# First product of two experts in the second token part: seven products of halves in place of eight

## The chip, the core and the metric

The program runs on one core of a Trainium2 chip. The metric is the device time of one execution in microseconds (us); before the change the median of three runs is 1135.14 us (1130.4 to 1138.75). The engines named here are PE (TensorE, the matmuls), DVE (VectorE), ACT (ScalarE), POOL (GpSimd) and SP (the queue that issues the transfers).

## What is computed

Attention over 4 batches and 8 heads gives a matrix `x` of 2304 tokens by 512. Then four experts and a last block work on it:

```python
p = domain_probs / (domain_probs.sum(-1, keepdims=True) + 1e-09)
out = np.zeros((N, D), dtype=np.float32)
for e in range(E):                       # 4 experts
    h = np.maximum(x @ w1[e], 0.0)       # first product, 512 -> 1024
    out += p[:, e:e + 1] * (h @ w2[e])   # second product, 1024 -> 512
# then: h = x @ w_in; SoLU and layer norm; @ w_out
```

## The kernel before

The 2304 tokens are 18 tiles of 128. Tiles 0 to 5 are the first part, tiles 6 to 17 the second; the second part is cut into four groups of three tiles, 384 tokens each (`GROUPS`). Every matrix is held as two f16 pieces, a high and a low one, and a product of two matrices is three matmuls: high times high, high times low, low times high.

The experts run in phases `j` = 0 to 7: phases 0 to 3 are the four experts on the first part, 4 to 7 the four experts on the second. Phases 0 to 4 run beside the attention, which ends in phase 4. Phase 5 is the second expert and phase 6 the third, both on the second part; phase 7 is the fourth, and the last block follows.

One group of one phase is two stretches. In the first, `emit_h` (matmul in line 310) makes 8 chunks of 128 hidden units by 384 tokens, each 4 slices of the inner dimension times three matmuls: 96 matmuls of 384 columns. A chunk has a PSUM bank (tile `hps`); ACT takes its positive part into the high half of a tile `hch` (line 318), and DVE writes the low half (line 319). In the second stretch `emit_o` (line 330) makes, for each of three token tiles, 24 matmuls of 512 columns into a bank `ops`, and DVE adds the result into `acc` (line 354; in the first expert ACT writes it, line 349, with a small scale `c` that DVE makes in line 374 into one of three buffers).

The weights of phase j+1 are loaded and split in phase j: `next_w` returns the loads and the splits, four of each per matrix (ACT line 263, DVE line 266, 1024 columns each), and `spread` mixes them among the units of a phase. The weights of the last block, `w_in` and `w_out`, come as 64-bit words, so DVE first turns them into 32-bit floats (lines 189 to 213) in buffers of a pool `cv`; a sum of their squares then goes through a small reduction (DVE line 246, matmul line 248).

A scheduler orders the instructions of each engine from this program order and from priorities (`tc.high_priority`); each engine then works in its order. PSUM has 8 banks: 3 in the pool `psh` and, from phase 5 on, 5 in the pool `psb`, taken in turn.

Of the kernel before, what the change touches and what calls it, by code (L numbers as in the profile page):

```python
# [14 lines left out]
AF = mybir.ActivationFunctionType  # L15
ALU = mybir.AluOpType
# [3 lines left out]
NB, NH, S, HD = 4, 8, 576, 64  # L20
NT, D, F, E = 2304, 512, 1024, 4
KD, KF = D // 128, F // 128
# [3 lines left out]
PRI = 2000  # L26
# [14 lines left out]
GROUPS = [[(0, 3), (3, 3)], [(6, 3), (9, 3), (12, 3), (15, 3)]]  # L41
NACC = 6
GT = 3
# [15 lines left out]
def tile_kernel(  # L59
# [16 lines left out]
    pe = nc.tensor  # L76
# [21 lines left out]
    vec, act, gp, sync = nc.vector, nc.scalar, nc.gpsimd, InOrder(nc.sync)  # L98
# [7 lines left out]
    hp = ctx.enter_context(tc.tile_pool(name="h", bufs=8))  # L106
# [51 lines left out]
    wt = {}  # L158
    cv = {}
# [129 lines left out]
    xT, x2T, acc = {}, {}, {}  # L289
# [9 lines left out]
    def emit_h(e, t0, k, fs, pool):  # L299

        g, c0 = group(t0)
        n = 128 * k
        ps = pool.tile([128, 512], F32, tag="h", name="hps")
        w, x = wt["w1", e], xT[g]
        h = hp.tile([128, 2, 128 * GT], F16, tag="h", name="hch")
        for j, f in enumerate(fs):
            m = 0
# [14 lines left out]

    def emit_o(e, o0, pool):

        ps = pool.tile([128, 512], F32, tag="h", name="ops")
        w = wt["w2", e]
        m = 0
        for f in range(KF):
            for a, b in ((0, 0), (0, 1), (1, 0)):
                pe.matmul(  # L330
                    ps, hch[f][:, a, o0:o0 + 128], w[:, b, f, :], start=(m == 0), stop=(m == 3 * KF - 1)
                )
                m += 1
        return ps
# [66 lines left out]
    def phase_units(j, runs, pool):  # L401

        e = j % E
        units = []
        for t0, k in runs:
            cost = 12 * (k * 128 / 2400 + 0.003)
            per = GT // k
            for f in range(0, KF, per):
                fs = range(f, min(f + per, KF))
                units.append((t0 + k - 1, lambda t=t0, k=k, fs=fs: emit_h(e, t, k, fs, pool), cost * len(fs)))  # L410
            for t in range(t0, t0 + k):
                units.append((
                    t, lambda t=t, o=(t - t0) * 128: out_unit(e, t, o, pool), 24 * 0.216,
                ))
        return units


    nw = [0]
# [619 lines left out]
    late.append(ctx.enter_context(tc.tile_pool(name="late", bufs=1)))  # L1038
    fetch()


    psbs = ExitStack()
    psb = psbs.enter_context(tc.tile_pool(name="psb", bufs=8 - NPH, space=PSUM))
    for j in range(5, 8):
        us = phase_units(j, GROUPS[1], psb)
        n = len(us) if j < 7 else len(us) * 3 // 4
        with ExitStack() as es:
            if j == 7:
                cv["pool"] = es.enter_context(tc.tile_pool(name="cv", bufs=2))
            pa, qa = next_w()  # L1050
            pb, qb = next_w()
            end = 0.9 * n if j < 7 else n
            for _, u, _ in spread(us[:n], (0, 0.1 * n, post), (0.1 * n, 0.5 * n, pa + qa), (0.5 * n, end, pb)):
                u()
        post = qb
    m = len(us) - n
    for _, u, _ in spread(us[n:], (m - 3.0, m - 0.5, post)):
        u()
# [170 lines left out]
```

## Time and profile before

| what | value |
|---|---|
| median of the runs | 1135.14 us |
| the profiled execution, its own time | 1134.88 us |
| its span, first to last instruction | 1132.9 us |
| outside of the span | 2.0 us |
| PE busy | 1072.2 us, 95% of the span |
| DVE busy | 708.8 us, 63% |
| ACT busy | 470.2 us, 42% |
| POOL busy | 184.5 us, 16%, none of it after about 430 us |
| first product (line 310) | 396.9 us of PE |
| second product (line 330) | 387.4 us of PE |
| phase 5 begins, phase 6 begins, phase 7 begins | 569.43, 692.20, 816.76 us |

Busy time counts the time in which an engine had an instruction running. "x" and a number is how many instructions a row puts together. "idle before" is the idle time of the engine ahead of these instructions, with what ended it.

### The profile page before, as it was taken

The page shows a single profiled execution, that of the slowest core. Times are in us where ns is not written, and L with a number is a line of the kernel's source. Part 1 is how long each engine was busy: PE and PEld are TensorE (multiplying, and loading weights), DVE is VectorE, ACT ScalarE, POOL GpSimd, SP SyncE. Part 2 cuts the span into 40 slices and gives each one's busy share as a digit, 9 for nine tenths or more (in the row PEclk, how much of TensorE's full clock was granted, in tenths as well). Part 3 has the DMA queues.
Part 4 walks back from the last instruction along what each step waited for, and adds up shares of the span by engine and source line. Part 5 has one row for each costly group of instructions (what it writes and reads, how often), then busy time and mean ns, then how long its engine had stood idle before and what let it go on. Part 6 is the DMA issues. An engine that isn't in the chain of part 4 may idle for free.

```text
span 1132.9 us, 18415 instructions
## 1 busy us (share of the span) xinstructions
PE 1072.2 (95%) x7200; PEld 608.7 (54%) x7200; DVE 708.8 (63%) x1530; ACT 470.2 (42%) x1003; POOL 184.5 (16%) x176
## 2 busy tenths in 40 slices
PE   4588889899998999999999999999999999999998
PEld 4456766466555656655555555555555554444443
DVE  7898778557677678535332225212788656999883
ACT  5566776646655466432321123111334342333222
POOL 4974633224125311000000000000000000000000
PEclk9999989899999999999999999999999999999999
DMA  9777986738649547324240004000232102343433
GB/s 322 218 170 160 239 200 156 218 81 230 155 95 267 135 127 194 73 42 138 80 144 1 1 1 149 1 1 1 76 93 84 37 21 29 75 103 75 84 84 84
DMA packets 216054, 125.75 MB, mean 111 GB/s; under 512 B 183712, under 2 KB 185760, under 8 KB 215456
## 3 DMA queue, kind: packets, MB, share of 16 engines
q1 hardware_dynamic: 215968, 124.59, 42.7%
q8 instruction: 56, 0.92, 0.3%
q14 instruction: 30, 0.25, 0.1%
HBM read 73.18 MB, written 6.29 MB: 70 GB/s over the span
## 4 chain that ended last, share of the span: by engine, by line
PE 78%; DMA 9%; DVE 5%; POOL 4%; issue 2%; ACT 1%; SPq 1%; POOLq 0%; ACTq 0%; DVEq 0%
PE ops L330 29%; PE hps L310 27%; PE h L1080 8%; PE o L1143 8%; DMA pT<-hl 6%; PE pv L683 2%; PE sps L610 1%; DMA vraw<-in_vC_dram 1%; DVE hl L654 1%; PE sps L611 1%; DVE nm L616 1%; POOL ks L493 1%; POOL wt L259 1%; ACT p L649 1%; POOL ks L491 1%
## 5 line engine op out<-in xcount | busy, mean ns | idle before, releaser
L310 PE MATMUL hps<-xT,wt 128*128 128x384 f16 (+1 forms) x2688 | 396.9, 307 | 2.2 <-DVE hch L319 1.2
L330 PE MATMUL ops<-wt,hch 128*128 128x512 f16 x1728 | 387.4, 381 | 2.5 <-DVE hch L319 1.3
L310 PEld LDWEIGHTS <-wt 128*128 128x128 f16 x2688 | 240.9, 100 | 137.7 <-issue 5.5
L330 PEld LDWEIGHTS <-hch 128*128 128x128 f16 x1728 | 167.4, 99 | 195.7 <-issue 6.5
L318 ACT ACTIVATE hch<-hps 128x384 f16<-128x384 f32 (+1 forms) x194 | 93.8, 484 | 257.5 <-PE hps L310 257.1
L319 DVE SCALAR_TENSOR_TENSOR hch<-hps,hch 128x384 f16<-128x384 f32 (+1 forms) x194 | 105.9, 548 | 124.2 <-ACT hch L318 124.1
L649 ACT ACTIVATE p<-sps,nm 128x320 f32<-128x320 f32 (+4 forms) x144 | 79.0, 553 | 88.5 <-DVE nm L620 55.2
L654 DVE TENSOR_TENSOR hl<-p,hl 128x320 f16<-128x320 f32 (+4 forms) x132 | 91.8, 708 | 30.3 <-ACT hl L653 30.0
L266 DVE SCALAR_TENSOR_TENSOR wt<-stage,ws,wt 128x1024 f16<-128x1024 f32 x72 | 97.0, 1367 | 21.2 <-ACT wt L263 19.8
L354 DVE SCALAR_TENSOR_TENSOR acc<-ops,coef,acc 128x512 f32<-128x512 f32 x54 | 40.4, 748 | 111.0 <-PE ops L330 111.0
L1080 PE MATMUL h<-wt,x2T 128*128 128x512 f16 x432 | 95.5, 379 | 0.8 <-DVE acc L354 0.8
L1143 PE MATMUL o<-wt,lt 128*128 128x512 f16 x432 | 95.5, 379 | 0.0
L610 PE MATMUL sps<-ks,qhi 128*128 128x288 f32 (+3 forms) x160 | 67.4, 424 | 19.0 <-ACT p L649 8.8
L263 ACT ACTIVATE wt<-stage,ws 128x1024 f16<-128x1024 f32 x64 | 70.6, 1141 | 16.0 <-PE ops L330 11.2
L683 PE MATMUL pv<-v,pT 128*128 128x64 f16 x1392 | 54.7, 197 | 17.2 <-DMA pT<-hl 17.2
L1080 PEld LDWEIGHTS <-x2T 128*128 128x128 f16 x432 | 42.2, 98 | 52.0 <-issue 1.1
L1143 PEld LDWEIGHTS <-lt 128*128 128x128 f16 x432 | 42.3, 98 | 50.9
L653 ACT ACTIVATE hl<-p 128x320 f16<-128x320 f32 (+4 forms) x132 | 65.9, 521 | 6.9 <-DMA pT<-hl 6.4
L683 PEld LDWEIGHTS <-pT 128*128 128x128 f16 x1392 | 49.5, 100 | 26.6 <-DMA pT<-hl 21.0
L1093 ACT ACTIVATE ex<-h,nb,cs 128x1024 f32<-128x1024 f32 x18 | 21.7, 1205 | 84.4 <-DVE nb L1090 43.6
L611 PE MATMUL sps<-ks,qlo 128*128 128x288 f32 (+3 forms) x160 | 52.2, 329 | 3.1 <-POOL qlo L493 3.1
L127 ACT ACTIVATE junk<-stage 128x1024 bf16<-128x1024 f32 x40 | 42.1, 1053 | 25.7 <-DMA stage<-in_w_dram 12.9
(130 smaller groups left out, 939.5 us busy)
## 6 DMA issues: line engine op xcount, KB each, us to landing
stage<-in_w_dram SPq DMA_DIRECT2D x64, 512.0 KB, 5.8
raw<-in_qT_dram SPq DMA_DIRECT2D x34, 256.0 KB, 3.6
vraw<-in_vC_dram SPq DMA_DIRECT2D x30, 256.0 KB, 3.2
raw<-in_kT_dram SPq DMA_DIRECT2D x24, 288.0 KB, 3.6
raw<-in_w_in_dram SPq DMA_DIRECT2D x4, 1024.0 KB, 6.0
raw<-in_w_out_dram SPq DMA_DIRECT2D x4, 1024.0 KB, 5.2
out_dram<-o2s SPq DMA_DIRECT2D x16, 256.0 KB, 2.0
raw<-in_kT_dram SPq DMA_DIRECT2D x8, 192.0 KB, 4.2
```

Of the source, the lines that this page charges most:

```text
L263: h = bg_(act.activation(out=hi, in_=r, func=AF.Copy, scale=stage[key, "s"]), "A")
L266: stage["last"] = vec.scalar_tensor_tensor(out=lo, in0=r, scalar=stage[key, "s"], in1=hi, op0=ALU.mult, op1=ALU.subtract)
L310: pe.matmul(ps[:, j * n:j * n + n], w[:, a, kk, f * 128:(f + 1) * 128], x[:, b * KD + kk, c0:c0 + n], start=(m == 0), stop=(m == 3 * KD - 1),)
L318: nc.scalar.activation(out=h[:, 0, :n], in_=ps[:, :n], func=AF.Relu)
L319: nc.vector.scalar_tensor_tensor(out=h[:, 1, :n], in0=ps[:, :n], scalar=0.0, in1=h[:, 0, :n], op0=ALU.max, op1=ALU.subtract)
L330: pe.matmul(ps, hch[f][:, a, o0:o0 + 128], w[:, b, f, :], start=(m == 0), stop=(m == 3 * KF - 1))
L610: pe.matmul(o, hi[:, h % 4], rhs, start=True, stop=False)
L649: act.activation(out=dst, in_=src, func=AF.Exp, bias=nm[:, j + x:j + x + 1], scale=SCALE, accum_out=sums[:, h:h + 1],)
L654: anc["D"] = vec.tensor_tensor(out=hl[:, W + c0:W + c0 + n_], in0=pf[:, 0:n_], in1=hl[:, c0:c0 + n_], op=ALU.subtract)
L683: pe.matmul(o, tt[:, a * nch + c, :], v[:, bb, hs], start=(m == 0), stop=(m == total - 1))
L1080: pe.matmul(ps[:, half], x[:, a * KD + kk, c:c + 128], w[:, b, kk, half * 512:half * 512 + 512], start=(m == 0), stop=(m == 3 * KD - 1),)
L1143: pe.matmul(ps, tt[:, a * KF + f], w[:, b, f], start=(m == 0), stop=(m == 3 * KF - 1))
```

## The change

In phases 5 and 6 the first product of a group, (1024 hidden by 512 inner) times (512 inner by 384 tokens), is cut in halves in all three dimensions and done by Strassen's scheme in Winograd's form: seven products of 512 by 256 by 192 in place of eight, with sums of halves ahead of them and behind them. Phase 7, phases 0 to 4 and all second products stay as they are.

- The hidden dimension is taken in two passes (`half` 0 and 1). A pass has seven products (`f1` to `f7`), each in one bank: 2 column halves `jj`, 2 inner slices, 3 matmuls, so 12 matmuls of 192 columns; a group has 14 products and 168 matmuls.
- Behind the products, `add` (DVE, seven per pass, 384 columns) and one ACT copy put them together in f32 tiles `stu` in SBUF; `hidden` takes the positive part (ACT, 192 columns, 8 per pass) and the low piece (DVE, 8 per pass).
- Ahead of the products, `t_steps` makes four sums `T` of the token halves, once per group of tokens, and `s_steps` four sums `S` of the weight halves, once per expert and pass. Each is 14 DVE instructions (384 columns for `T`, 512 for `S`) and 4 ACT copies. The sums of group 0 and of the second expert are put among the units that are left of phase 4 when the attention has been issued; `T` of the other groups and `S` of the third expert stand in phase 5.
- `T` and `S` lie in a pool `keep` and the f32 tiles in a pool `tmp`, both closed after phase 6; the pool `cv` is opened only then.
- The second products take the chunks in the order in which they were made (`for f in hch`), and in phases 5 and 6 their banks come from `psh`.

```diff
+    def combine(shape, out, x, y, op):
+        ...
+        def high():
+            r["f"] = view(st_["tmp"].tile([128, 512], F32, tag="f", name="stf", bufs=3))
+            vec.tensor_tensor(out=r["f"], in0=x(0), in1=y(0), op=op)
+
+        def low():
+            if y(1) is None:
+                vec.tensor_tensor(out=r["f"], in0=r["f"], in1=x(1), op=ALU.add)
+                return
+            if "l" not in r:
+                r["l"] = view(st_["tmp"].tile([128, 512], F32, tag="l", name="stl", bufs=1))
+                vec.tensor_tensor(out=r["l"], in0=x(1), in1=y(1), op=op)
+            vec.tensor_tensor(out=r["f"], in0=r["f"], in1=r["l"], op=ALU.add)
+
+        def split():
+            two_parts(r["f"], out(0), out(1))     # ACT copy to f16, DVE subtract
+        return r, [high, low, split]
+
+    def st_units(e, g, half, pool):
+        ...
+        def product(c, lhs, rhs):
+            ps[c] = pool.tile([128, 512], F32, tag="h", name="hps")
+            for jj in range(2):
+                m = 0
+                for kk in range(2):
+                    for a, b in ((0, 0), (0, 1), (1, 0)):
+                        pe.matmul(
+                            ps[c][:, jj * HT:jj * HT + HT], lhs(a, kk, jj), rhs(b, kk),
+                            start=(m == 0), stop=(m == 5),
+                        )
+                        m += 1
+        def add(k, x, y):
+            ...
+                vec.tensor_tensor(out=u[k], in0=x, in1=y, op=ALU.add)
+        def hidden(x, fs, j):
+            ...
+                    act.activation(out=h[:, 0], in_=v, func=AF.Relu)
+                    vec.scalar_tensor_tensor(
+                        out=h[:, 1], in0=v, scalar=0.0, in1=h[:, 0], op0=ALU.max, op1=ALU.subtract
+                    )
+        def f1():
+            ...
+            product(1, A(0, 0), B(0, 0))
+            ...
+                act.activation(out=u["b"], in_=ps[1][:, :W], func=AF.Copy)
+        def f2():
+            product(6, S(1), T(1))
+            add("u", u["b"], ps[6][:, :W])
+        def f3():
+            product(2, A(0, 1), B(1, 0))
+            add("s1", u["b"], ps[2][:, :W])
+            hidden(u["s1"], fa, 0)
+        def f4():
+            product(7, S(2), T(2))
+            add("v", u["u"], ps[7][:, :W])
+        def f5():
+            product(5, S(0), T(0))
+            add("s2", u["v"], ps[5][:, :W])
+            hidden(u["s2"], fb, 1)
+            add("w", u["u"], ps[5][:, :W])
+        def f6():
+            product(4, A(1, 1), T(3))
+            add("s3", u["v"], ps[4][:, :W])
+            hidden(u["s3"], fb, 0)
+        def f7():
+            product(3, S(3), B(1, 1))
+            add("s4", u["w"], ps[3][:, :W])
+            hidden(u["s4"], fa, 1)
+    ...
-        for f in range(KF):
+        for f in hch:
...
-    while moe:
-        moe.pop()[1]()
...
+    for _, u, _ in spread(moe, (0, len(moe), t_steps(0) + s_steps(1, 0) + s_steps(1, 1))):
+        u()
...
-    for j in range(5, 8):
-        us = phase_units(j, GROUPS[1], psb)
+    for j in (5, 6):
+        ...
+        tasks = [post + pa[:5], pa[5:] + qa, [], pb]
+        if first:
+            for g in range(3):
+                tasks[g] = t_steps(g + 1) + tasks[g]
+        for _, u, _ in st_phase(e, psb, psh, tasks, [s_steps(e + 1, h) for h in range(2)] if first else None):
+            u()
+    sts.close()
+    us = phase_units(7, GROUPS[1], psb)
```

On PE, at the head of the first group of phase 5, a chunk of the kernel before is 12 pairs of a weight load and a matmul of 384 columns (`hps` is the bank, `wt` the weights, `xT` the tokens; `ops_7415` is the last second product of phase 4):

```order
L330 MATMUL ops_7415<-wt_6128,hch_7336 128x512
L310 LDWEIGHTS wt_6684
L310 MATMUL hps_7473<-xT_2313,wt_6684 128x384
L310 LDWEIGHTS wt_6684
L310 MATMUL hps_7489<-xT_2313,wt_6684 128x384
```

In the changed kernel, at the ninth product of the same group (of 12 pairs of 192 columns), there stands:

```order
L529 LDWEIGHTS S_7356
L529 MATMUL hps_7718<-T_7046,S_7356 128x192
L331 LDWEIGHTS hch_7554
L331 MATMUL ops_7844<-wt_7774,hch_7554 128x512
...
L331 LDWEIGHTS hch_7555
L331 MATMUL ops_7844<-wt_7774,hch_7555 128x512
L529 LDWEIGHTS wt_6684
L529 MATMUL hps_7738<-xT_2313,wt_6684 128x192
```

The matmuls are half as wide, and in this first group some of the second product's matmuls (`ops_7844`, six here) stand between the first products.

On DVE, behind the last chunk `hch_7149` of phase 4's third group, the kernel before has the conversion of `w_in` and then that of the next chunks (`cvA`, `cvP` are its words). The changed kernel has there the sums of group 0 (`stf`, `stl` are the f32 tiles, `xT_2313` the tokens of group 0, `T_7046` their sums):

```order
L320 SCALAR_TENSOR_TENSOR hch_7149<-hps_7148,hch_7149 128x384
L437 TENSOR_TENSOR stf_7063<-xT_2313 128x384
L445 TENSOR_TENSOR stl_7065<-xT_2313 128x384
L446 TENSOR_TENSOR stf_7063<-stf_7063,stl_7065 128x384
L437 TENSOR_TENSOR stf_7090<-xT_2313,stf_7063 128x384
L445 TENSOR_TENSOR stl_7166<-xT_2313 128x384
L425 TENSOR_TENSOR T_7046<-stf_7063,T_7046 128x384
L441 TENSOR_TENSOR stf_7090<-stf_7090,xT_2313 128x384
L437 TENSOR_TENSOR stf_7127<-xT_2313,stf_7090 128x384
L437 TENSOR_TENSOR stf_7164<-xT_2313 128x384
L425 TENSOR_TENSOR T_7046<-stf_7090,T_7046 128x384
L441 TENSOR_TENSOR stf_7127<-stf_7127,xT_2313 128x384
```

Four rows on comes the first of three small scales (`c0`, line 374 before), then the sums of the second expert's weights. The conversion of `w_in` has moved behind phase 6.

On DVE, further on in phase 5's first group, the adds that empty the banks (`stu<-stu,hps`) stand among the sums of the last group (`T_8349`, tokens `xT_6125`) and the splits of the third expert's first weights (`wt_8209`):

```order
L548 SCALAR_TENSOR_TENSOR hch_7555<-stu_7602,hch_7555 128x192
L541 TENSOR_TENSOR stu_7643<-stu_7626,hps_7630 128x384
L541 TENSOR_TENSOR stu_7649<-stu_7586,hps_7630 128x384
L541 TENSOR_TENSOR stu_7667<-stu_7626,hps_7654 128x384
L266 SCALAR_TENSOR_TENSOR wt_8209<-stage_7870,ws_7872,wt_8209 128x1024
L425 TENSOR_TENSOR T_8349<-stf_8450,T_8349 128x384
L441 TENSOR_TENSOR stf_8504<-stf_8504,xT_6125 128x384
L266 SCALAR_TENSOR_TENSOR wt_8209<-stage_7870,ws_7872,wt_8209 128x1024
L446 TENSOR_TENSOR stf_8594<-stf_8594,stl_8622 128x384
L266 SCALAR_TENSOR_TENSOR wt_8209<-stage_7870,ws_7872,wt_8209 128x1024
L541 TENSOR_TENSOR stu_7688<-stu_7649,hps_7675 128x384
L541 TENSOR_TENSOR stu_7731<-stu_7714,hps_7718 128x384
```

Before the change DVE had there only the eight chunks of the group and four splits. `hps_7675` is the seventh product of the group; the twelfth, `hps_7775`, takes its bank.

## Rows read from the trace of the kernel before

**Rows 1.** The page: busy time, and the slices of PE, DVE and the granted clock.
```profile
PE 1072.2 (95%) x7200; PEld 608.7 (54%) x7200; DVE 708.8 (63%) x1530; ACT 470.2 (42%) x1003; POOL 184.5 (16%) x176
...
PE   4588889899998999999999999999999999999998
...
DVE  7898778557677678535332225212788656999883
...
PEclk9999989899999999999999999999999999999999
```

**Rows 2.** Busy time in phases 5, 6, 7: PE, PEld, DVE, ACT, POOL, clock.
```profile
569.40:692.20 122.80, 122.80 (x662) 64.69 (x661) 35.35 (x52) 24.35 (x41) 0.00 (x0) 1.00 0.13 42
692.20:816.80 124.60, 124.60 (x674) 65.77 (x673) 42.83 (x59) 26.20 (x44) 0.00 (x0) 1.00 0.09 34
816.80:942.60 125.80, 124.96 (x677) 66.15 (x676) 88.55 (x159) 45.53 (x85) 0.00 (x0) 1.00 0.22 58
```

**Rows 3.** Timeline of PE: start, length, line, form, count.
```profile
537.32 16.74 PE L310 MATMUL hps<-xT,wt 128*128 128x384 f16 x102
553.89 15.70 PE L330 MATMUL ops<-wt,hch 128*128 128x512 f16 x72
569.43 13.98 PE L310 MATMUL hps<-xT,wt 128*128 128x384 f16 x85
...
692.20 15.76 PE L310 MATMUL hps<-xT,wt 128*128 128x384 f16 x96
707.80 15.70 PE L330 MATMUL ops<-wt,hch 128*128 128x512 f16 x72
723.34 15.76 PE L310 MATMUL hps<-xT,wt 128*128 128x384 f16 x96
```

**Rows 4.** Timeline of PE: runs of short matmuls beside the attention.
```profile
98.09 5.25 PE L310 MATMUL hps<-xT,wt 128*128 128x128 f16 x91
...
370.74 1.04 PE L683 MATMUL pv<-v,pT 128*128 128x64 f16 x30
```

**Rows 5.** Groups of PE and its weight loads: count, busy us, mean ns of one.
```profile
L310 PE MATMUL hps<-xT,wt 128*128 128x128 f16 x576 | 41.3, 232 | 1.0 <-DMA xT<-xh 1.0
L310 PEld LDWEIGHTS <-wt 128*128 128x128 f16 x2688 | 240.9, 100 | 137.7 <-issue 5.5
L683 PEld LDWEIGHTS <-pT 128*128 128x128 f16 x1392 | 49.5, 100 | 26.6 <-DMA pT<-hl 21.0 <-issue 0.9
```

**Rows 6.** Groups of DVE and ACT by form: count, busy us, mean ns.
```profile
L319 DVE SCALAR_TENSOR_TENSOR hch<-hps,hch 128x384 f16<-128x384 f32 x188 | 103.5, 553 | 124.2 <-ACT hch L318 124.1
L213 DVE TENSOR_TENSOR stage<-stage,cvA 128x1024 f32<-128x1024 f32 x8 | 9.6, 1217 | 0.0
L318 ACT ACTIVATE hch<-hps 128x384 f16<-128x384 f32 x188 | 91.5, 487 | 256.7 <-PE hps L310 256.4
L393 ACT ACTIVATE xh<-acc,xs 128x512 f16<-128x512 f32 x18 | 12.9, 717 | 6.7 <-DVE xs L138 5.4 <-DVE xi L131 1.4
```

**Rows 7.** Timeline of DVE in phase 7, where instructions follow without a gap.
```profile
859.84 2.47 DVE L266 SCALAR_TENSOR_TENSOR wt<-stage,ws,wt 128x1024 f16<-128x1024 f32 x2
862.23 1.01 DVE L319 SCALAR_TENSOR_TENSOR hch<-hps,hch 128x384 f16<-128x384 f32 x2
...
865.89 2.35 DVE L213 TENSOR_TENSOR stage<-stage,cvA 128x1024 f32<-128x1024 f32 x2
868.16 1.67 DVE L236 TENSOR_SCALAR stage<-stage,gl 128x512 f32<-128x512 f32 x4
```

**Rows 8.** Timeline of ACT and DVE around the end of the attention.
```profile
520.36 0.69 DVE L189 TENSOR_SCALAR cvA<-raw 128x1024 int32<-128x1024 int32 x1 [0.94 <-DMA raw<-in_w_in_dram]
...
521.16 0.49 ACT L318 ACTIVATE hch<-hps 128x384 f16<-128x384 f32 x1 [1.46 <-PE hps L310]
...
529.03 0.69 DVE L205 TENSOR_SCALAR cvP<-cvA 128x1024 int32<-128x1024 int32 x1
...
538.29 0.27 DVE L374 TENSOR_SCALAR c<-pt,iw 128x1 f32<-128x1 f32 x1 [4.96 <-ACT acc L349]
```

**Rows 9.** Timeline of DVE and PE in phase 7: the reduction of `w_in`.
```profile
833.73 0.15 DVE L246 TENSOR_REDUCE wt<-wt 128x1 f32<-128x4 f32 x1
...
853.75 0.28 PE L248 MATMUL tp<-wt,ones 128*128 128x1 f32 x2
```

More of the change, by code (lines that the diff above doesn't have):

```diff
@@ L306, in emit_h @@
         for j, f in enumerate(fs):
+            hch.pop(f, None)
             m = 0
@@ L415, in phase_units, with two_parts, view @@
         return units
+    HT = 64 * GT
+    st_ = {}
+    Ts, Ss = {}, {}
+    def two_parts(x, hi, lo):
+        act.activation(out=hi, in_=x, func=AF.Copy)
+        vec.tensor_tensor(out=lo, in0=x, in1=hi, op=ALU.subtract)
+    def combine(shape, out, x, y, op):
+        n = shape[0] * shape[1]
+        r = {}
+        def view(f):
+            return f[:, :n].rearrange("p (a b) -> p a b", a=shape[0])
+        def high():
[12 more added lines that the diff above has]
+        return r, [high, low, split]
@@ new lines, in t_steps, with B, T, place @@
+    def t_steps(g):
+        X = xT[1, g]
+        def B(i, j):
+            return lambda b: X[:, b * KD + 2 * i:b * KD + 2 * i + 2, HT * j:HT * j + HT]
+        def T(k):
+            return lambda b: Ts[g][:, k, b]
+        def place():
+            Ts[g] = st_["keep"].tile([128, 4, 2, 2, HT], F16, tag=f"T{g}", name="T")
+        sh = (2, HT)
+        r1, a1 = combine(sh, T(0), B(0, 1), B(0, 0), ALU.subtract)
+        r2, a2 = combine(sh, T(1), B(1, 1), lambda b: None if b else r1["f"], ALU.subtract)
+        r3, a3 = combine(sh, T(2), B(1, 1), B(0, 1), ALU.subtract)
+        r4, a4 = combine(sh, T(3), B(1, 0), lambda b: None if b else r2["f"], ALU.subtract)
+        return [place] + a1 + a2 + a4 + a3
@@ new lines, in s_steps, with A, S, place @@
+    def s_steps(e, half):
+        def A(i, j):
+            return lambda b: wt["w1", e][:, b, 2 * j:2 * j + 2, 512 * i + 256 * half:512 * i + 256 * half + 256]
+        def S(k):
+            return lambda b: Ss[e, half][:, k, b]
+        def place():
+            Ss[e, half] = st_["keep"].tile([128, 4, 2, 2, 256], F16, tag=f"S{half}", name="S")
+        sh = (2, 256)
+        r1, a1 = combine(sh, S(0), A(1, 0), A(1, 1), ALU.add)
+        neg = lambda b: None if b else r1["f"]
+        r2 = {}
+        def second():
+            r2["f"] = st_["tmp"].tile([128, 512], F32, tag="f", name="stf", bufs=3).rearrange("p (a b) -> p a b", a=2)
+            vec.tensor_tensor(out=r2["f"], in0=r1["f"], in1=A(0, 0)(0), op=ALU.subtract)
+        def second_low():
+            vec.tensor_tensor(out=r2["f"], in0=r2["f"], in1=A(0, 0)(1), op=ALU.subtract)
+        def second_split():
+            two_parts(r2["f"], S(1)(0), S(1)(1))
+        r3, a3 = combine(sh, S(2), A(0, 0), A(1, 0), ALU.subtract)
+        r4, a4 = combine(sh, S(3), A(0, 1), lambda b: None if b else r2["f"], ALU.subtract)
+        return [place] + a1 + [second, second_low, second_split] + a4 + a3
@@ new lines, in st_units, with A, S, B @@
+    def st_units(e, g, half, pool):
+        key = (1, g)
+        t = GROUPS[1][g][0] + GT - 1
+        fa = [2 * half, 2 * half + 1]
+        fb = [4 + f for f in fa]
+        ps, u = {}, {}
+        def A(i, j):
+            return lambda a, kk, jj: wt["w1", e][:, a, 2 * j + kk, (4 * i + fa[jj]) * 128:(4 * i + fa[jj] + 1) * 128]
+        def S(k):
+            return lambda a, kk, jj: Ss[e, half][:, k, a, kk, jj * 128:jj * 128 + 128]
+        def B(i, j):
+            return lambda b, kk: xT[key][:, b * KD + 2 * i + kk, HT * j:HT * j + HT]
+        def T(k):
+            return lambda b, kk: Ts[g][:, k, b, kk]
+        def product(c, lhs, rhs):
[9 more added lines that the diff above has]
+                        m += 1
+        W = 2 * HT
+        def add(k, x, y):
+            n = {"s": 3, "u": 2}.get(k[0], 1)
+            u[k] = st_["tmp"].tile([128, W], F32, tag=k[0] + str(n), name="stu", bufs=n)
+            with tc.high_priority(offset=PRI):
+                vec.tensor_tensor(out=u[k], in0=x, in1=y, op=ALU.add)
+        def hidden(x, fs, j):
+            with tc.high_priority(offset=PRI):
+                for jj, f in enumerate(fs):
+                    h, v = hch[f][:, :, HT * j:HT * j + HT], x[:, jj * HT:jj * HT + HT]
+                    act.activation(out=h[:, 0], in_=v, func=AF.Relu)
[3 more added lines that the diff above has]
+        def f1():
+            for f in fa + fb:
+                hch.pop(f, None)
+                hch[f] = hp.tile([128, 2, 128 * GT], F16, tag="h", name="hch")
+            product(1, A(0, 0), B(0, 0))
+            u["b"] = st_["tmp"].tile([128, W], F32, tag="b1", name="stu", bufs=1)
+            with tc.high_priority(offset=PRI):
+                act.activation(out=u["b"], in_=ps[1][:, :W], func=AF.Copy)
[22 more added lines that the diff above has]
+            hidden(u["s4"], fa, 1)
+        return [(t, f, 0.0) for f in (f1, f2, f3, f4, f5, f6, f7)]
@@ new lines, in st_phase @@
+    def st_phase(e, pool, opool, tasks, end):
+        us = []
+        for g, (t0, k) in enumerate(GROUPS[1]):
+            gs = st_units(e, g, 0, pool) + st_units(e, g, 1, pool)
+            outs = [(t, lambda t=t, o=(t - t0) * 128: out_unit(e, t, o, opool), 0.0) for t in range(t0, t0 + k)]
+            n = len(gs)
+            if g == len(GROUPS[1]) - 1 and end:
+                gs = spread(gs[:n // 2], (0, n // 2, tasks[g])) + spread(gs[n // 2:] + outs, (0, 5, end[0]), (5, 10, end[1]))
+            else:
+                gs = spread(gs + outs, (1, n + 3, tasks[g]))
+            us += gs
+        return us
@@ L1043, in tile_kernel @@
     psb = psbs.enter_context(tc.tile_pool(name="psb", bufs=8 - NPH, space=PSUM))
-    for j in range(5, 8):
-        us = phase_units(j, GROUPS[1], psb)
[L1046 to L1054, printed above, removed]
-        post = qb
+    for j in (5, 6):
+        pa, qa = next_w()
+        pb, qb = next_w()
+        e = j % E
+        first = j == 5
+        tasks = [post + pa[:5], pa[5:] + qa, [], pb]
[4 more added lines that the diff above has]
+            u()
+        post = qb
+    sts.close()
+    us = phase_units(7, GROUPS[1], psb)
+    n = len(us) * 3 // 4
+    with ExitStack() as es:
+        cv["pool"] = es.enter_context(tc.tile_pool(name="cv", bufs=2))
+        pa, qa = next_w()
+        pb, qb = next_w()
+        for _, u, _ in spread(us[:n], (0, 0.1 * n, post), (0.1 * n, 0.5 * n, pa + qa), (0.5 * n, n, pb)):
+            u()
+    post = qb
     m = len(us) - n
```

4 lines of the change are left out of this document (added).

## The prediction

> **What bounds the kernel now.** I began with the busy shares and the slices of the page [rows 1]: PE is busy 95% of the span, in tenths 9 or more in nearly every slice from the tenth on, and its granted clock is at nine tenths or above. DVE is at 1 to 5 tenths where phases 5 and 6 lie (slices 21 to 28). Then the busy times by phase [rows 2]: in phases 5 and 6 PE is busy in every microsecond (122.80 of 122.80, 124.60 of 124.60) at the upper clock, 2.4 GHz, while DVE works 35.35 and 42.83 us and ACT 24.35 and 26.20. So these two phases are PE alone, and a shorter PE stream shortens them as long as DVE, which gets the new work, keeps up. Last the timeline of PE [rows 3]: in the first group of phase 6 the first product starts at 692.20, the second at 707.80, the next group at 723.34: 15.60 + 15.54 = 31.14 us a group, with no gap. Eight such groups make phases 5 and 6.
>
> **What PE gains.** Before: 15.60 us for 96 matmuls of 384 columns is 162.5 ns each, 160 of it at one column a cycle of 2.4 GHz, so 2.5 ns are fixed. After: 168 matmuls of 192 columns. No such width stands in the trace, but its neighbours do [rows 4]: 91 matmuls of 128 columns, each with its own weights, take 5.25 us. Less the 0.23 us that one matmul takes [rows 5], that is 5.02/90 = 55.8 ns, again 2.5 over 53.3. 30 matmuls of 64 columns take 1.04 us; less about 0.2 for the last, 29 ns. So 192 columns cost 80 + 2.5 = 82.5 ns, a product of twelve 0.99 us, a group 168 x 0.0825 = 13.86 us in place of 15.60. The gain is 1.74 us a group, **13.9 us** in eight.
>
> That holds only if weight loads stay hidden, since there are 168 in place of 96 and a load lasts 100 ns by itself [rows 5], longer than the matmul. The same group of rows says that loads overlap: 1392 loads of the 64-column matmuls, 100 ns each, fill only 49.5 us, 36 ns each. Against that stands the Trainium skill (TensorE: Matmul & The Clock Gate, section Back-to-back issue gap): in a real stream of load and matmul pairs it gives about 81 ns for 128 columns and 131 for 512, and calls the formula that fits these rows an isolated gap that under-counts. By these figures 192 columns would be about 89 ns (an estimate on the line between them) and the gain only 0.6 us a group; the trace has 56 ns in such a stream at 128, so it does not bear the page out here.
>
> **What DVE gets.** Its price list first. DVE instructions that follow each other start before the last one has ended [rows 7]: of two `hch` writes of 0.55 us (384 columns) the pair takes 1.01, so the second starts 0.46 after the first; a pair of weight splits of 1.28 takes 2.47, so 1.19; two adds of 1024 columns from SBUF take 2.35, so 1.13. From 384 to 1024 columns a whole duration grows from 0.553 to 1.217 [rows 6], 1.04 ns a column. Adds of 384 and 512 columns with two operands are not in the trace; the nearest rows give 0.46 and 0.59 us from start to start, 0.55 and 0.69 as whole durations; 192 columns 0.26 and 0.35. A cheaper end is the single-operand scaling of 512 columns: four take 1.67, 0.42 each [rows 7]. I take 0.46, 0.59, 0.26.
>
> A pass has 7 adds and 8 low pieces: 7 x 0.46 + 8 x 0.26 = 5.3 us of DVE against 7 x 0.99 = 6.9 of PE. With five banks PE may run four products ahead. ACT has one copy and 8 pieces, by its row of 487 ns for 384 columns [rows 6] under 4 us. So in a group without extra work nothing holds PE up, and the 1.74 us stand. The last pieces of a group are hidden by its second product, which starts with the chunks of the first pass (12 matmuls of 0.216 = 2.6 us for each token tile).
>
> The extra work is the sums. `T` costs 14 x 0.46 = 6.4 us a group, `S` 14 x 0.59 = 8.3 us a pass, with their ACT copies (0.49 to 0.72 us by its rows [rows 6]) beside it. The order shows where they stand: from the last chunk of phase 4's third group on, DVE has the sums of group 0, both passes of the second expert, then `T` of groups 1 to 3, all ahead of or among the first group's adds. This queue can begin at about 522.2: that chunk's ACT half ends at 521.65 [rows 8], DVE's 0.46 later. Up to the add that empties bank `hps_7675` I count 111 instructions: 69 of 384 columns (54 of them in sums, 8 `hch`, 7 bank adds), 28 of 512, 8 weight splits, 2 of 192 and 4 small ones: 31.7 + 16.5 + 9.5 + 0.5 + 0.8 = 59.1 us. The three small scales wait on ACT, the last until 538.29 [rows 8]; the queue reaches it about then anyway.
>
> PE meanwhile: phase 4 and its order stay, only the few matmuls of phase 5 that are mixed into it change. Before, 11 matmuls of 384 columns (1.79 us) are done when phase 5 begins at 569.43 (85 of the 96 are left [rows 3]); now 35 of 192 (2.89 us), so phase 4 ends at 570.5. After one more matmul at 570.6 the third product, `hps_7589`, is whole. DVE reaches its add at 570.0 (19 instructions with 11.3 us are left of the 59.1) and waits until 570.8 with 0.2 us of passing on. It then empties `hps_7675` at 570.8 + 11.3 = 582.1. PE needs that bank for the twelfth product after 6 more products, 6 matmuls of 512 columns and 2 products: 570.6 + 5.9 + 1.3 + 2.0 = 579.8. So **PE stalls 2.3 us** there. What is behind (33 instructions, 13 us of DVE, up to 595.5) runs beside 21 us of PE work and is not waited for again.
>
> The other dense place is the end of phase 5 and the first group of phase 6: two passes of `S` (16.6 us) and eight splits (9.5) are added to the bank work. From the second product of phase 5's last group to the last low piece of the next group DVE has 91 instructions of 44.3 us; PE has 13.86 + 15.54 + 13.86 of products and 2.6 of second products ahead of the first one that needs that piece, 45.9, less 2 at the start. Even, with margins of about 1 us at single banks: I set down **0.5 us**.
>
> Moved: the conversion of `w_in` did ten of its instructions, 9 us, from 520.36 to 529.7 [rows 8] beside the attention's end, and now comes wholly after the last product of phase 6, since `cv` takes the place of `keep`. In the kernel before the reduction that ends it stands at 833.73, its matmul at 853.75 [rows 9], 20 us of cover; the shift takes 9 us of it or a little more, so it is hidden. Without that cover PE would stop at that matmul, some microseconds at most. The transfers stay as many, and SP has nothing else late.
>
> **Sum** against the profiled execution: 1134.9 - 13.9 + 2.3 + 0.5 = 1123.8. The median of the runs is 0.3 above that execution, so **1124 us**, a ratio of 0.990.
>
> **Rivals.**
> - *DVE pays whole durations* (each sum waits for what it reads to be written). The same queue is 69 x 0.55 + 28 x 0.69 + 8 x 1.28 + 1.5 = 69.0 us, its end 591.2, the stall 11.4; the dense place at the end of phase 5 loses about 5 more (57 instructions by 0.09). 1134.9 - 13.9 + 16.4 = 1137, slightly slower. For it: sums that read the one before. Against it: in the order other instructions stand between nearly all such pairs. Half of it gives 1130. Chance of half or more 0.20.
> - *Weight loads set the pace*, 100 ns a pair [rows 5]: 16.8 us a group in place of 15.60, 8 x 1.2 = 9.6 us lost, nothing to stall: 1144, **slower**. It decides from 15.60/168 = 92.9 ns a matmul on. Against it are the runs at 29 and 56 ns. Chance 0.05.
> - *No stall to speak of*: sums at 0.42 us and less, then DVE waits for PE's products and only the splits among the adds (4 x 1.19) hold PE up, 1 us: 1122. Chance 0.15.
> - *Every pass stalls a little*, since product, add, ACT and DVE are a chain with 5 banks: 0.5 us in 16 passes, 8 us: 1131. The busy shares speak against it (5.3 of 6.9). Chance 0.08.
> - *Phase 7 stalls* for the later conversion, 2 to 6 us: 1128. Chance 0.05.
>
> The forecast itself has 0.47.
>
> **How the numbers follow.** About 1% is what a measurement of this kernel can tell from no change, that is 11.4 us, or 1123.8: the forecast lies on that edge. Faster by over 1%: two fifths of the forecast's 0.47 and most of the third rival, 0.19 + 0.13 = 0.32, with a little for the spread of runs 0.36. Slower by over 1% (1146.5): the weight loads with their spread, and mishaps of two rivals together, 0.05. Within 1%: 0.59. The range goes from 1119 (no stall, less 2 us of spread of the runs) to 1134 (the first rival at three quarters); outside lie the first rival's end and the weight loads, some 0.15 with mishaps. The likeliest case alone has 1121 to 1127.
>
> **What would show it.** Matmuls of 192 columns start 82 to 83 ns apart; more than 93 would make the prediction wrong. A quiet group of phase 5 or 6 takes 29.4 us. PE's idle time in phases 5 and 6 is 2 to 4 us, nearly all in one gap near 580, ended by a bank add of DVE; gaps in every group would be the fourth rival. DVE is busy without a break from 522 to about 580, and a sum of 384 columns starts 0.46 us after the one before; 0.55 is the first rival. The reduction of `w_in` comes before its matmul is reached.

## The result and the profile after

Runs taken in turn on one chip: the kernel before has a median of 1134.78 us (4 runs, 1130.4 to 1138.75), the changed one 1121.97 us (4 runs, 1120.33 to 1123.12). The ratio is 0.988, 95% interval 0.986 to 0.990, so the change makes the kernel 1.2% faster, 12.8 us by the medians. The prediction was 1124 us with a range from 1119 to 1134.

The profiled execution of the changed kernel took 1120.33 us, its span is 1118.5 us. The page's busy times and the slices of DVE answer to [rows 1]:

```profile
PE 1054.0 (94%) x7776; PEld 642.1 (57%) x7776; DVE 821.9 (73%) x1818; ACT 500.8 (45%) x1115; POOL 184.7 (17%) x176
...
DVE  6888787648678678536997459544999656999883
```

PE has 18 us less to do with 576 matmuls more; DVE has 113 us more. Where DVE stood at 1 to 5 tenths before (slices 21 to 28), it stands at 4 to 9 now; the peaks are slices 20 to 22 (531 to 615 us) and 25.

Busy time by stretch, in the columns of [rows 2]: the end of phase 4 from the first output product of its third group on, then phases 5, 6 and 7.

```profile
518.79:567.95 49.16, 49.16 (x273) 25.98 (x272) 48.59 (x91) 22.54 (x39) 0.00 (x0) 1.00 0.22 72
567.95:685.50 117.55, 115.78 (x956) 82.93 (x955) 82.03 (x175) 36.39 (x91) 0.00 (x0) 1.00 0.13 44
685.50:802.36 116.86, 116.86 (x933) 81.39 (x932) 73.20 (x154) 31.98 (x81) 0.00 (x0) 1.00 0.12 45
802.36:928.20 125.84, 125.00 (x678) 66.14 (x677) 94.46 (x166) 47.42 (x89) 0.00 (x0) 1.00 0.25 74
```

Phase 5 takes 117.55 us where it took 122.80, phase 6 116.86 where it took 124.60; phase 7 is as long as before. PE still fills both phases but for 1.77 us in phase 5. The first stretch has DVE busy in 48.59 of 49.16 us: this is the queue of sums.

Nearly all of what PE loses is in one place. PE's timeline there (start, length, line, form, count, and in brackets the idle time ahead with what ended it):

```profile
575.26 1.15 PE L529 MATMUL hps<-xT,wt 128*128 128x192 f16 x12
576.25 2.14 PE L529 MATMUL hps<-T,S 128*128 128x192 f16 x24
578.23 0.59 PE L331 MATMUL ops<-wt,hch 128*128 128x512 f16 x2
580.45 1.15 PE L529 MATMUL hps<-T,wt 128*128 128x192 f16 x12 [1.62 <-DVE stu L541]
```

and DVE's, with the queue that the bank's sum stood in:

```profile
574.85 1.28 DVE L266 SCALAR_TENSOR_TENSOR wt<-stage,ws,wt 128x1024 f16<-128x1024 f32 x1
576.05 0.55 DVE L425 TENSOR_TENSOR T<-stf,T 128x384 f16<-128x384 f32 x1
576.52 0.55 DVE L441 TENSOR_TENSOR stf<-stf,xT 128x384 f32<-128x384 f32 x1
576.99 1.28 DVE L266 SCALAR_TENSOR_TENSOR wt<-stage,ws,wt 128x1024 f16<-128x1024 f32 x1
578.18 0.55 DVE L446 TENSOR_TENSOR stf<-stf,stl 128x384 f32<-128x384 f32 x1
578.65 1.28 DVE L266 SCALAR_TENSOR_TENSOR wt<-stage,ws,wt 128x1024 f16<-128x1024 f32 x1
579.85 1.01 DVE L541 TENSOR_TENSOR stu<-stu,hps 128x384 f32<-128x384 f32 x2
```

Three weight splits for the next expert and three pieces of the `T` sums of a later group run from 574.85 to 579.85; only then come two bank sums. The first of them, by the order in "The change", empties `hps_7675` and ends at about 580.4, and PE starts at 580.45. That PE had to wait for it can be read in the list of PE's waits from 505 us to the end (engine, line, releaser: us in all, times, longest; a second gap of 0.3 us, which the list doesn't name, comes up with the experiments):

```profile
PE hps L529 <- DVE stu L541: 1.6, 1, 1.6
PE h L1283 <- DVE acc L355: 0.8, 1, 0.8
```

The second wait stands in the kernel before as well.

**A yardstick for all kernels.** The attention part at the start varies from execution to execution (below). So the kernels are compared from the first output product of phase 4's third group (the mark) to the first output product of phase 7, both of which can be read off PE's timeline as runs of 72 matmuls. Such runs stand in [rows 3] too. The two ends, before and after:

```profile
521.78 15.70 PE L330 MATMUL ops<-wt,hch 128*128 128x512 f16 x72
...
832.36 15.70 PE L330 MATMUL ops<-wt,hch 128*128 128x512 f16 x72
```
```profile
518.79 15.70 PE L331 MATMUL ops<-wt,hch 128*128 128x512 f16 x72
...
817.96 15.70 PE L331 MATMUL ops<-wt,hch 128*128 128x512 f16 x72
```

That is 310.58 us before and 299.17 us after, 11.41 less. From there to the end of the span both have 300.54 us.

One correction belongs to the yardstick. In both kernels five matmuls of phase 5 run ahead of the mark, directly behind the 96 of phase 4's third group (60 earlier, then 36). Before they are long ones, so that 41 stand together; in the changed kernel they are short (as they are in the last experiment, which shortens the matmuls of phases 5 and 6 alone):

```profile
515.11 6.83 PE L310 MATMUL hps<-xT,wt 128*128 128x384 f16 x41
```
```profile
512.53 6.01 PE L311 MATMUL hps<-xT,wt 128*128 128x384 f16 x36
...
518.38 0.58 PE L529 MATMUL hps<-xT,wt 128*128 128x192 f16 x5
```

So 0.81 us of phase 5's work lay ahead of the mark before and 0.41 us after, and the stretch falls by 5 x (0.1625 - 0.0825) = 0.40 us less than the work does. The change thus won 11.4 + 0.4 = 11.8 us in phases 5 and 6.

### The profile page after: what moved, and what is told of

Its sections match the earlier page's. It is cut to its first block, busy times and chain, and to the rows that moved or that the text cites. A ratio compares the mean times of both kernels' runs of the same rounds, so it can differ in the third digit from the quotient of the medians.

```text
span 1118.5 us, 19987 instructions
## 1 busy us (share of the span) xinstructions
PE 1054.0 (94%) x7776; PEld 642.1 (57%) x7776; DVE 821.9 (73%) x1818; ACT 500.8 (45%) x1115; POOL 184.7 (17%) x176
## 4 chain that ended last, share of the span: by engine, by line
PE 73%; DVE 11%; DMA 8%; POOL 4%; issue 3%; ACT 1%; SPq 0%; DVEq 0%; ACTq 0%; POOLq 0%
PE ops L331 27%; PE hps L311 15%; PE hps L529 9%; PE h L1283 8%; PE o L1346 8%; DMA pT<-hl 6%; PE pv L872 3%; DVE wt L266 2%; DVE hl L843 1%; PE sps L799 1%; PE sps L800 1%; DVE stf L437 1%; DMA vraw<-in_vC_dram 1%; POOL wt L259 1%; DVE hch L320 1%
## 5 line engine op out<-in xcount | busy, mean ns | idle before, releaser
L311 PE MATMUL hps<-xT,wt 128*128 128x384 f16 (+1 forms) x1920 | 268.5, 297 | 1.7 <-DVE hch L320 1.3
L311 PEld LDWEIGHTS <-wt 128*128 128x128 f16 x1920 | 164.0, 100 | 85.9 <-issue 4.0
L266 DVE SCALAR_TENSOR_TENSOR wt<-stage,ws,wt 128x1024 f16<-128x1024 f32 x72 | 99.7, 1392 | 8.3 <-ACT wt L263 6.9
L319 ACT ACTIVATE hch<-hps 128x384 f16<-128x384 f32 x130 | 62.3, 482 | 75.1 <-PE hps L311 74.6
L320 DVE SCALAR_TENSOR_TENSOR hch<-hps,hch 128x384 f16<-128x384 f32 x130 | 70.5, 544 | 32.2 <-ACT hch L319 32.2
L541 DVE TENSOR_TENSOR stu<-stu,hps 128x384 f32<-128x384 f32 x112 | 59.4, 550 | 17.3 <-PE hps L529 17.3
L547 ACT ACTIVATE hch<-stu 128x192 f16<-128x192 f32 x128 | 39.2, 354 | 70.4 <-DVE stu L541 70.2
L529 PEld LDWEIGHTS <-S 128*128 128x128 f16 x768 | 64.3, 98 | 2.6
```

Source lines behind the costliest of these rows:

```text
L266: stage["last"] = vec.scalar_tensor_tensor(out=lo, in0=r, scalar=stage[key, "s"], in1=hi, op0=ALU.mult, op1=ALU.subtract)
L311: pe.matmul(ps[:, j * n:j * n + n], w[:, a, kk, f * 128:(f + 1) * 128], x[:, b * KD + kk, c0:c0 + n], start=(m == 0), stop=(m == 3 * KD - 1),)
L320: nc.vector.scalar_tensor_tensor(out=h[:, 1, :n], in0=ps[:, :n], scalar=0.0, in1=h[:, 0, :n], op0=ALU.max, op1=ALU.subtract)
L529: pe.matmul(ps[c][:, jj * HT:jj * HT + HT], lhs(a, kk, jj), rhs(b, kk), start=(m == 0), stop=(m == 5),)
```

## The experiments

Four questions are open after this profile: whether the attention part, 3.0 us shorter, belongs to the gain; whether the sums cost anything but this one wait, and whether it is their place or their amount that costs; whether the gain comes by the group; and what a 192-column matmul costs by itself. The last column is the stretch of the yardstick. Each ratio is to runs of the kernel before on the same chip; their median was 1134.78 us (4 runs) beside the first profile of the changed kernel, 1134.12 (17) beside the last two kernels of the table and 1135.93 (11) beside the others. The ratios come with the measurement and are not the quotients of these medians.

| kernel | median us (runs) | ratio to before, interval | stretch us |
|---|---|---|---|
| before, first profile | 1134.78 (4) | | 310.58 |
| before, second profile | 1139.96 (1) | | 310.59 |
| changed, first profile | 1121.97 (4) | 0.988, 0.986 to 0.990 | 299.17 |
| changed, second profile | 1121.97 (5) | 0.990, 0.986 to 0.993 | 299.16 |
| later sums held back | 1119.18 (4) | 0.986, 0.983 to 0.988 | 297.07 |
| no sums | 1120.5 (6) | 0.987, 0.985 to 0.990 | 297.07 |
| 14 sums more | 1122.71 (5) | 0.988, 0.986 to 0.991 | 298.88 |
| seven products in phase 6 alone | 1126.95 (6) | 0.994, 0.992 to 0.996 | 303.62 |
| eight products, matmuls halved | 1135.7 (12) | 1.002, 1.000 to 1.003 | 312.91 |

### Both kernels once more

> The changed kernel once more, for a second profile. Theory (the gain sits in phases 5 and 6 alone, and the 3.0 us by which the attention part was shorter in the first profile are chance between executions): from the first output product of phase 4's third group to the start of phase 7 it takes 283.6 us again within 0.4, with one wait of 1.6 us on the sum that empties a bank in group 0 of phase 5, while the attention part ahead of it may end anywhere between 518 and 523 us. Rival (the change shortens the attention part too): that part ends at 518.8 within 0.5 again. Time 1120 to 1123 us.

> The kernel before once more, for a second profile. Theory (the attention part varies from execution to execution): it ends (first output product of phase 4's third group) up to 4 us away from 521.8 us, while from there to the start of phase 7 it takes 295.0 us within 0.4 and from there to the end 316 us within 0.6. Rival: it ends at 521.8 us within 0.5 again.

For the stretch both expectations held: it came out at 299.16 and 310.59 us, each within 0.01 of the first profile; to the start of phase 7 it was 283.56 where 283.6 was expected, and 294.99 where 295.0 was. The bounds on the attention part missed: the mark stood at 523.82 for the changed kernel, beyond the 523 allowed (518.79 in its first profile), and at 526.81 for the kernel before, 5.0 us and not up to 4 from 521.78. So the same program ends its attention part 5 us earlier or later, and the rivals, which had it end at the same moment again, fall.

Whose the 3.0 us are is less clear, since the second profiles differ by 3.0 us again. That they are the change's is unlikely: up to the mark the two kernels' traces hold the same instructions in the same order on PE, DVE, ACT and POOL, but for the five matmuls above and two conversions of `w_in`. The other kernels with the changed start reach the mark at 519.63, 525.15 and 523.63 us, those with the old one at 521.82 and 524.15. A small effect isn't excluded by so few profiles; the gain claimed here is the stretch's alone.

What differs beside it in the changed kernel is the granted clock. Busy time from 100 to 200 us, columns as in [rows 2] (the clock is third from the end), first the changed kernel's two profiles, then the two of before:

```profile
100.00:200.00 100.00, 88.11 (x1032) 65.72 (x1028) 80.77 (x161) 69.10 (x170) 45.96 (x42) 0.97 0.82 193
```
```profile
100.00:200.00 100.00, 89.95 (x1020) 66.42 (x1017) 78.41 (x160) 67.09 (x165) 43.17 (x40) 0.93 0.80 183
```
```profile
100.00:200.00 100.00, 87.25 (x1026) 65.16 (x1023) 81.15 (x164) 70.13 (x173) 45.70 (x42) 0.96 0.83 195
```
```profile
100.00:200.00 100.00, 89.62 (x1027) 66.23 (x1023) 79.46 (x162) 67.73 (x167) 43.16 (x41) 0.95 0.83 188
```

The changed kernel's means, 0.97 and 0.93, come from time spent at the lower of the two levels, 1.2 in place of 2.4 GHz, and with 0.93 fewer matmuls were done in the same 100 us (1020 for 1032). But the two profiles of before, just as far apart at the mark, have 0.96 and 0.95 there, with as many matmuls (1026 and 1027). So the clock in this stretch doesn't explain their 5 us, and what does stays open.

### The later sums held back

The first instruction of the `T` sums of the third and fourth group gets a same-engine order behind the last bank sum of the group two before:

```diff
     def t_steps(g):
...
+        def pin():
+            a1[0]()
+            if ("s4", g - 2) in last:
+                after(r1["i"], last["s4", g - 2])
...
-        return [place] + a1 + a2 + a4 + a3
+        return [place, pin] + a1[1:] + a2 + a4 + a3
...
-                vec.tensor_tensor(out=u[k], in0=x, in1=y, op=ALU.add)
+                last[k, g] = vec.tensor_tensor(out=u[k], in0=x, in1=y, op=ALU.add)
```

> The T sums of the third and fourth group are held on VectorE behind the last sum of the group two before theirs, so that 28 of them (about 13 us at 0.47 us each) no longer stand in the queue ahead of the sum that PE waits for. Theory (the 1.6 us stall is queue order on VectorE, nothing else): the wait goes, no new one of over 0.3 us takes its place, and the time falls by 1.6 us against the changed kernel (1120.4 if that is 1122.0). Rival (the next bank or the weights' conversion is late next): a wait of 1 to 2 us shows elsewhere in phase 5 and the time stays within 0.5 us.

The wait is gone and no other came. PE's timeline at the same place, and the two ends of the stretch:

```profile
575.80 1.15 PE L535 MATMUL hps<-T,S 128*128 128x192 f16 x12
576.79 0.38 PE L331 MATMUL ops<-wt,hch 128*128 128x512 f16 x1
577.01 1.15 PE L535 MATMUL hps<-T,S 128*128 128x192 f16 x12
578.00 1.46 PE L331 MATMUL ops<-wt,hch 128*128 128x512 f16 x6
579.29 1.15 PE L535 MATMUL hps<-T,wt 128*128 128x192 f16 x12
```
```profile
519.63 15.70 PE L331 MATMUL ops<-wt,hch 128*128 128x512 f16 x72
...
816.70 15.70 PE L331 MATMUL ops<-wt,hch 128*128 128x512 f16 x72
```

The stretch is 2.10 us shorter (299.17 to 297.07), more than the 1.6 expected. The list of waits had shown only part of the loss: from start to start PE lost 1.78 us at the wait (two matmuls of 512 columns from 578.23 on would have ended the turn at 578.66, and the next began at 580.45), and the other 0.3 us go in a second, smaller gap that the list doesn't name. It lies in the changed kernel's ten output matmuls from 583.29 on, which would have been over at 585.45 at 0.216 us each:

```profile
583.29 2.64 PE L331 MATMUL ops<-wt,hch 128*128 128x512 f16 x10
585.77 1.15 PE L529 MATMUL hps<-xT,wt 128*128 128x192 f16 x12
```

The median is 1119.18 us, 2.8 below the changed kernel's; the intervals of the two ratios overlap, so the step between them rests on the stretch. It is the fastest version of the study.

### No sums at all

`t_steps` and `s_steps` return nothing, and the products read pieces of `xT` and `wt` in place of `T` and `S`:

```diff
-            return lambda a, kk, jj: Ss[e, half][:, k, a, kk, jj * 128:jj * 128 + 128]
+            return A(k // 2, k % 2)
...
-            return lambda b, kk: Ts[g][:, k, b, kk]
+            return B(k // 2, k % 2)
```

> Left out: all T and S sums and their splits (112 VectorE and 32 ScalarE instructions); the products take pieces of the inputs and weights of the same shape in their place, so the output is not the reference's. Theory (the sums cost only the one stall): 1.6 us less than the changed kernel, 8 groups of 29.4 us each and no PE wait in phases 5 and 6. Rival (the sums cost more than the stall that shows, by slowing the products or the attention part): more than 2.5 us less, with products of 192 columns faster than 0.99 us for 12. Rival (the stall is not the sums'): the wait stays.

The two ends of the stretch:

```profile
525.15 15.70 PE L331 MATMUL ops<-wt,hch 128*128 128x512 f16 x72
...
822.22 15.70 PE L331 MATMUL ops<-wt,hch 128*128 128x512 f16 x72
```

That is 297.07 us, the same to the hundredth as with the later sums held back, and 2.10 us less than the changed kernel where 1.6 was expected. So 112 sums and splits on DVE and 32 copies on ACT cost the kernel nothing by their amount; all that they cost in the change as made is the 2.10 us of those two gaps. The rival with more than 2.5 us falls. Without `T` and `S` in the names the 168 matmuls of a group are one row:

```profile
644.08 15.70 PE L331 MATMUL ops<-wt,hch 128*128 128x512 f16 x72
659.62 14.02 PE L529 MATMUL hps<-xT,wt 128*128 128x192 f16 x168
673.48 15.70 PE L331 MATMUL ops<-wt,hch 128*128 128x512 f16 x72
```

13.86 us from start to start, 82.5 ns a matmul.

### Fourteen sums more

```diff
-    for _, u, _ in spread(moe, (0, len(moe), t_steps(0) + s_steps(1, 0) + s_steps(1, 1))):
+    for _, u, _ in spread(moe, (0, len(moe), t_steps(0) + s_steps(1, 0) + s_steps(1, 1) + t_steps(0, 3) + [lambda: st_.update(extra=st_["lo"])])):
```

(`t_steps(0, 3)` writes group 0's sums into group 3's place. The bank sum is also ordered behind them; as many sums stand ahead of it as before: the traces of both kernels have the same 111 instructions there.)

> 14 more T sums and splits on VectorE (group 0's once more, into the place that group 3's fill later), emitted with the first ones, 6.6 us of VectorE work. In the order of VectorE's instructions nothing changes ahead of the sum that PE waits for: the 14 push as many later sums behind it. Theory (the place in the queue decides, not the amount of work): the stall stays at 1.6 us within 0.4, the queue runs without a break for 6 to 7 us longer, and the time is that of the changed kernel within 0.5 us, unless the second half of group 0 comes late: then at most 6.6 us more. Rival (VectorE's amount of work counts from where the queue starts): 6.6 us more, 1128.6.

The wait is as long as before:

```profile
585.27 1.15 PE L531 MATMUL hps<-T,wt 128*128 128x192 f16 x12 [1.60 <-DVE stu L543]
```

The stretch is 298.88 us, 0.29 less than without the extra work and not 6.6 more (the median is 0.7 us above the changed kernel's, within the spread): the amount of DVE's work isn't what counts. The 0.29 us are the second small gap, which nearly closes here; behind the bank sum 384-column sums stand where 512-column ones stood, so the rest of the queue there passes 0.13 us a piece sooner. One part of the expectation missed: DVE's first break comes 89.3 us behind the mark (612.91) in place of 75.6 (594.39), 13.7 us later and not 6 to 7; that the next group's bank sums joined the queue meanwhile would explain it, but wasn't followed up. PE has no wait from that either.

How the wait grows when the bank sum itself is put later was not tried.

### Seven products in phase 6 alone

```diff
-    for j in (5, 6):
...
+    us = phase_units(5, GROUPS[1], psb)
...
+    sums = sum([t_steps(g) for g in range(4)], []) + s_steps(2, 0) + s_steps(2, 1)
+    for _, u, _ in spread(us, (0, 0.1 * n, post), (0.1 * n, 0.5 * n, pa + qa), (0.5 * n, 0.9 * n, pb), (0.55 * n, n, sums)):
+        u()
...
+    for _, u, _ in st_phase(2, psb, psh, [post + pa[:5], pa[5:] + qa, [], pb], None):
+        u()
```

> Phase 5 multiplies as before (eight products, 384 columns); phase 6 alone uses seven products of halves. The T sums of all four groups and the third expert's S sums are spread over the second half of phase 5, where VectorE had 35 us of work in 123. Theory (the gain is 1.74 us a group by matmul count, and the stall came from the crowded VectorE queue at the start of phase 5): 4 x 1.74 = 6.96 us less than the kernel before, no PE wait in phases 5 and 6, 1127.8 us beside 1134.8. Rival (each pass of seven products pays a wait of its own, or phase 6's gain leans on phase 5's): 4 us less or fewer.

Exactly the theory: the stretch is 303.62 us, 6.96 less than before, and PE waits for nothing from 505 to 835 us. The two ends of the stretch:

```profile
521.82 15.70 PE L331 MATMUL ops<-wt,hch 128*128 128x512 f16 x72
...
825.44 15.70 PE L331 MATMUL ops<-wt,hch 128*128 128x512 f16 x72
```

The gain comes by the group, 1.74 us in each, and neither a product nor a pass pays a wait of its own. The median fell by 7.2 us.

### Eight products with matmuls of half the width

The kernel before with each matmul of phases 5 and 6 cut in two, `parts` being 2 there and 1 elsewhere:

```diff
+            q = n // parts
+            for p in range(parts):
+                m = 0
...
-                        ps[:, j * n:j * n + n], w[:, a, kk, f * 128:(f + 1) * 128], x[:, b * KD + kk, c0:c0 + n],
+                            ps[:, j * n + p * q:j * n + p * q + q], w[:, a, kk, f * 128:(f + 1) * 128],
+                            x[:, b * KD + kk, c0 + p * q:c0 + p * q + q],
```

> The kernel before with each 384-column matmul of phases 5 and 6 cut into two of 192 columns: the same eight products, 192 matmuls and 192 weight loads a group in place of 96, no sums. Theory (a matmul takes 0.417 ns a column and 2.5 ns, weight loads hidden): a group's first product 15.84 us in place of 15.60, 8 x 0.24 = 1.9 us more than the kernel before. Rival (a load and matmul pair cannot go below 100 ns): 19.2 us a group, 29 us more. Rival (isolated gap, 89 ns a matmul): 17.1 us a group, 12 us more.

```profile
695.94 16.00 PE L312 MATMUL hps<-xT,wt 128*128 128x192 f16 x192
711.78 15.70 PE L333 MATMUL ops<-wt,hch 128*128 128x512 f16 x72
```

15.84 us from start to start, as reckoned to the hundredth; twice the weight loads are free. The stretch is 2.33 us longer, 1.92 of it the eight groups and 0.4 the five matmuls at the mark as above. The time is up by a ratio of 1.002 (1.000 to 1.003), 1.6 us by the medians. Both rivals, 12 and 29 us, fall. (The 89 ns of the second is called an isolated gap there by mistake; it is the prediction's estimate for a stream of load and matmul pairs.)

## Why the prediction was right

**The matmul.** 82.5 ns from the neighbours at 64, 128 and 384 columns was exact (13.86 us in 168, 15.84 us in 192). The stretch gives the 13.9 us back: without a wait it is 310.58 - 297.07 = 13.51 us shorter, and 13.91 with the 0.40 at the mark. The rival of the weight loads is out. From the mark to phase 7 the 192-column matmuls fill 115.37 us and their loads 111.33; that isn't a sign that the loads were near their limit, since loads of 100 ns that follow each other every 82.5 ns overlap and fill nearly all the time:

```profile
518.79:802.36 283.57, 115.37 (x1341) 111.33 (x1339) 1.00 0.14 49
```

The Trainium skill (TensorE: Matmul & The Clock Gate, section Back-to-back issue gap) gives figures for a stream of load and matmul pairs by which I had estimated 89 ns at this width; the runs don't bear that out, 82.5 ns is what the same section calls the isolated gap.

**The wait.** 2.3 us were forecast; by the kernel without sums it was 2.10, of which 1.78 at the place named and 0.3 in the gap behind it. The mechanism is the one named: DVE's queue of sums, still unbroken, with the sum that empties bank `hps_7675` too far back. But two of the numbers in it were off, and they nearly cancelled. DVE emptied the bank 61.6 us behind the mark, where the prediction had 582.1 - 521.78 = 60.3. And PE came to need it at 578.66, 59.9 us behind the mark, where 579.8 - 521.78 = 58.0 was reckoned: it was not the twelfth but the thirteenth product that waited, one product and two output matmuls later (0.99 + 0.43 us). So the twelfth did not take the bank of `hps_7675`, as "The change" has it; I had counted the banks round in order, and they seem to be handed out as they come free, which no run shows. A difference of two such moments, each some 60 us after the mark, was known to about 2 us at best, so the good figure has luck in it.

**DVE's prices.** A step of 0.46 us was taken for a sum of 384 columns and 0.59 for 512. The start of the queue shows 0.47 and, where a sum reads what the one directly ahead of it wrote, 0.59:

```profile
519.77 0.56 DVE L437 TENSOR_TENSOR stf<-xT 128x384 f32<-128x384 f16 x1
520.25 0.55 DVE L445 TENSOR_TENSOR stl<-xT 128x384 f32<-128x384 f16 x1
520.84 0.56 DVE L446 TENSOR_TENSOR stf<-stf,stl 128x384 f32<-128x384 f32 x1
521.43 0.56 DVE L437 TENSOR_TENSOR stf<-xT,stf 128x384 f32<-128x384 f16 x1
521.90 0.55 DVE L445 TENSOR_TENSOR stl<-xT 128x384 f32<-128x384 f16 x1
```

The count of 111 instructions up to the bank's sum was exact. They took 60.6 us (519.77 to 580.40) where 59.1 were reckoned: 0.01 us on each of the 97 of 384 and 512 columns is 1.0, and five such pairs, 0.12 us later each, make up the rest. The queue began 0.6 us later behind the mark, and the 0.8 us for which the prediction had DVE wait at the third product's bank did not come, as it had no break there. 1.5 + 0.6 - 0.8 are the 1.3 us by which DVE was late. The Trainium skill (Vector Engine (DVE) Microarchitecture Reference, section Measured stream behaviour on trn2) gives 1.0417 ns a column and about 75 ns an instruction. That makes 0.475 us by estimate for 384 columns; the trace agrees with its 0.47. The first rival, whole durations everywhere (0.55 us, 1137 us in all), is out: only where an instruction reads what the one directly ahead wrote is the step that long, and the order has few such pairs.

**The second dense place.** 0.5 us were set down, none came: between 600 us and phase 7 PE has no wait. I had reckoned 44.3 us of DVE beside 45.9 less 2, which was even; single waits did not form out of it.

**Moved and untouched.** The conversion of `w_in` is hidden. The reduction that ends it starts at 828.03, 11.3 us ahead of its matmul, where the kernel before had 20.0 us [rows 9]; the shift took 8.7 us of this cover, about the 9 reckoned. The matmul stands 37.0 us behind the start of phase 7 in both kernels, and PE doesn't wait for it:

```profile
828.03 0.15 DVE L246 TENSOR_REDUCE wt<-wt 128x1 f32<-128x4 f32 x1
```
```profile
839.35 0.28 PE L248 MATMUL tp<-wt,ones 128*128 128x1 f32 x2
839.49 6.82 PE L311 MATMUL hps<-xT,wt 128*128 128x384 f16 x41
```

DVE works 94.46 us in phase 7 where it worked 88.55, and the phase is as long as before; the rival of a stall there is out, as is the one of a small stall in every pass.

**The sum.** The forecast was 13.9 - 2.3 - 0.5 = 11.1 us less, the kernel won 13.9 - 2.1 = 11.8. So 1134.9 - 11.8 = 1123.1; the last 1.1 us to the median of 1121.97 are less than the spread of the runs. Where they come from isn't shown; the attention part, whose end moves by 5 us between executions, is the likeliest place, and the sum can't hold it. The forecast lay on the edge between "within 1%" (0.59) and "faster by over 1%" (0.36); the time fell just on the faster side, so the smaller chance came true, by 0.7 us of sum and 1.1 that the sum doesn't hold.

## What to carry to other kernels

When a change takes work from the engine that is the bound and gives a lot of small work to one that has room, the amount is not the first thing to fear: here 113 us more on DVE were free but for one place in its queue, which cost 2.1. Look for the moment at which urgent instructions stand behind work that isn't needed for long, and hold that work back: two order edges got the whole loss back. To see it, compare both kernels between two marks inside the stream of the bound engine, and count what crossed the marks; here that gave differences to 0.01 us where the whole time varies by several.

## What the runs showed of the hardware

- A matmul with its own weights takes 0.417 ns a column and 2.5 ns at 192 columns too: 82.5 ns, in runs of 168 and 192, while a load by itself is recorded at 100 ns [rows 5].
- On DVE a sum starts 0.47 us after the one ahead of it (384 columns) and 0.12 us later, at 0.59, when it reads the result of the instruction directly ahead; the recorded duration is 0.55 in both cases.
- The same program reached the same mark at 518.79 and at 523.82 us, and the one before the change at 521.78 and 526.81, while the 299 us (before: 311) from that mark to phase 7's first output product repeat to 0.01 us. The granted clock between 100 and 200 us was 0.97 and 0.93 in the first pair, 0.96 and 0.95 in the second, so it doesn't account for both.
